# Second dense layer, first half: each weight piece multiplied with two column groups in turn

## The chip, the cores and the metric

The kernel runs on one core of one Trainium2 chip. The metric is the device time of one execution in microseconds. The median of 3 runs before the change is 705.27 us (703.19 to 706.97).

## The reference

Three stages follow each other: attention over a window of 128 keys (batch 4, 8 heads, 576 positions, head size 64), a layer of experts that sends each token to one of 8 experts, and a dense layer. The change lies in the dense layer, which computes on x (2304 tokens by 512):

```python
def _moe2_ref(x, w1, w2, w3, w_out) -> np.ndarray:
    h = np.maximum(np.maximum(x @ w1, x @ w2), x @ w3)
    return (h @ w_out).astype(np.float32)
```

w1, w2 and w3 are 512 by 768, w_out is 768 by 512. They come as float64, and are converted on the core.

## The kernel before

The tokens are worked on in two halves of 1152. For each half the expert layer (`layer1`, two units a half) fills the tile yT, and `layer2(h, ...)` runs the dense layer on it. `layer2` cuts its half into three items of C2 = 384 columns (column groups) and steps the generator `moe2` through them: inner(0), inner(1), outer(0), inner(2), outer(1), outer(2).

*inner(x)* goes over the K2 = 6 blocks m of 128 hidden features, and over the three matrices i. One pair (m, i) is a **product**: 12 matmuls into one bank of PSUM (4 blocks of the 512 inputs, times 3 passes over the high and low f16 parts, each matmul with a weight load of its own and 384 columns). The pool psM has 4 such banks. The result is moved out of PSUM into a tile hx: for i = 0 by ScalarE (L1167), for i = 1 and 2 by VectorE, which takes the maximum with the hx before it (L1169). After i = 2 ScalarE writes the high f16 part of h (L1175) and GpSimd the low part (L1176, yh<-hx,yh). The tag hx has 4 buffers.

*outer(x)* multiplies h with w_out (L1190), scales the rows on ScalarE (L1196) and scatters them to the output (L1197).

The weights of this layer come in 24 pieces of 512 KB: 18 for the pairs (m, i), 6 for w_out. Class `Weights2` handles them. A piece is loaded as int32 words by a transfer on SyncE's queue into a buffer st2 (4 of them; L1065, and L1071 for w_out). VectorE then builds float32 from the words, two pieces at a time, in three steps of two instructions: L1105, L1110, L1116 (the profile shows b<-st and b<-st,b). One call of `tick` emits one step, so three ticks convert a pair of pieces. When the third step is emitted, the transfers for the pair after next are emitted too; they wait until VectorE has released the buffers. `finish` emits, for one piece, ScalarE's scaling and its high f16 part (L1133, L1134), and GpSimd's low part (L1135, g<-b,g or wo<-b,wo). The work is written out in program order and each engine runs its own instructions in that order, so what `tick` emits ahead of a product stands ahead of that product's hx on VectorE. Before each product inner emits ticks by this rule:

```python
for i in range(3):
    if w.done < 3 * (m + 2):
        w.tick()
        w.tick()
    w.tick()
    w.finish()
```

That is three ticks while fewer pieces are converted than two blocks m ahead need, and one tick else; a tick does nothing while more than three converted pieces wait for `finish`.

Each yield of `moe2` returns to `layer2`, which for half 0 advances the gathers of the tokens of the second half (`begin`, `turn`): GpSimd's indirect transfers xg<-xs (L877), ScalarE's and VectorE's split xc<-xg (L899, L900) and SyncE's transposing transfers xh<-xc (L907).

Of the kernel before, what the change touches and what calls it, by code (L numbers as in the profile page):

```python
# [7 lines left out]
F32 = mybir.dt.float32  # L8
# [3 lines left out]
ACTF = mybir.ActivationFunctionType  # L12
ALU = mybir.AluOpType
# [18 lines left out]
KD, KF, K2 = DM // 128, FF // 128, F2 // 128  # L32
# [15 lines left out]
def windowed_attention_moe_kernel(  # L48
# [16 lines left out]
    nc = tc.nc  # L65
# [6 lines left out]
    psM = ctx.enter_context(tc.tile_pool(name="psM", bufs=4, space=PSUM))  # L72
# [4 lines left out]
    xs = [dram.tile([HALF, DM], F32, name=f"xs{h}") for h in range(2)]  # L77
# [171 lines left out]
    fill = Fill()  # L249


    class Attention:
# [26 lines left out]
        def turn(self, nm, b, t, eng=None):  # L279
            a, n = self.raw.pop((nm, b, t)), self.rows(t)  # L280
            ps = psM.tile([128, 4, 128], F32, name="m", tag="m")
            for i in range(4):
                nc.tensor.transpose(  # L283
                    ps[:, i, 0:n], a[0:n, 2 * i:2 * i + 2].rearrange("p h d -> p (h d)"),
                    ident[0:n, 0:n],
                )
            if nm == "k":
                if not t:
                    self.kT[b] = self.p.tile([128, 4, S], F32, name="kT", tag="kT", bufs=2)
                o = self.kT[b][:, :, 128 * t:128 * t + n]  # L290
            else:
                self.qT[b, t] = self.p.tile([128, 4, 128], F32, name="qT", tag="qT", bufs=3)
                o = self.qT[b, t][:, :, 0:n]
            if eng:
                eng.tensor_copy(o, ps[:, :, 0:n])
            else:
                nc.scalar.activation(out=o, in_=ps[:, :, 0:n], func=ACTF.Copy)
# [615 lines left out]
    PASSES = ((0, 0), (0, 1), (1, 0))  # L913
# [130 lines left out]
    class Weights2:  # L1044
# [32 lines left out]
        def begin(self):  # L1077
            g = self.pool.tile([128, 6 * K2 * KD * 128], F16, name="g", tag="g", bufs=1)
            self.g = g.rearrange("p (l i m k c) -> p l i m k c", l=2, i=3, m=K2, k=KD)
# [56 lines left out]

    C2 = 384

    def moe2(pool, items, w, hmt, n2=C2, **kw):

        hms = hmt[:, 0:4 * K2 * C2].rearrange("p (s a f n) -> p s a f n", s=2, a=2, f=K2)
        hms = hms[:, :, :, :, 0:n2]

        def inner(x, yT, c, *_):
            ys = [yT[:, l, :, c:c + n2] for l in range(2)]
            hm = hms[:, x % 2]
            for m in range(K2):
                w.convert(3 * m + 3)
                run = None
                for i in range(3):  # L1150
                    if w.done < 3 * (m + 2):
                        w.tick()
                        w.tick()
                    w.tick()
                    w.finish()
                    ps = psM.tile([128, 512], F32, name="m", tag="m")[:, 0:n2]
                    n = 0
                    for kk in range(KD):
                        for wl, xl in PASSES:
                            nc.tensor.matmul(  # L1160
                                out=ps, lhsT=w.g[:, wl, i, m, kk, :],
                                rhs=ys[xl][:, kk, :], start=(n == 0), stop=(n == 3 * KD - 1),
                            )
                            n += 1
                    nx = pool.tile([128, C2], F32, name="hx", tag="hx", bufs=4)[:, 0:n2]
                    if i == 0:
                        nc.scalar.activation(out=nx, in_=ps, func=ACTF.Copy, scale=2.0 ** -6)  # L1167
                    else:
                        nc.vector.scalar_tensor_tensor(  # L1169
                            out=nx, in0=ps, scalar=2.0 ** -6, in1=run, op0=ALU.mult, op1=ALU.max  # L1170
                        )
                    run = nx
                    fill()
                    fill()
                nc.scalar.activation(out=hm[:, 0, m], in_=run, func=ACTF.Copy)  # L1175
                nc.gpsimd.tensor_tensor(  # L1176
                    out=hm[:, 1, m], in0=run, in1=hm[:, 0, m], op=ALU.subtract
                )
                yield

        def outer(x, yT, c, idxs, gates):
            w.convert(w.n)
            hm = hms[:, x % 2]
            for u in range(n2 // 128):
                t = c // 128 + u
                ps = psM.tile([128, 512], F32, name="m", tag="m")
                n = 0
                for f in range(K2):
                    for wl, xl in PASSES:
                        nc.tensor.matmul(  # L1190
                            out=ps, lhsT=hm[:, xl, f, 128 * u:128 * u + 128],
                            rhs=w.wo[:, wl, f, :], start=(n == 0), stop=(n == 3 * K2 - 1),
                        )
                        n += 1
                ob = pool.tile([128, DM], F32, name="ob", tag="ob", bufs=2)
                nc.scalar.activation(out=ob, in_=ps, func=ACTF.Copy, scale=gates[:, t:t + 1])  # L1196
                nc.gpsimd.indirect_dma_start(  # L1197
                    out=out[:, :],
                    out_offset=bass.IndirectOffsetOnAxis(ap=idxs[:, t:t + 1], axis=0),
                    in_=ob[:, :], in_offset=None, **kw,  # L1200
                )
                yield

        for x, item in enumerate(items):
            yield from inner(x, *item)
            if x:
                yield from outer(x - 1, *items[x - 1])
        yield from outer(len(items) - 1, *items[-1])

    def rest(pool, m2, xT, yT, w, hmt):  # L1210
# [11 lines left out]
        with tc.For_i(0, nx, 1) as i:  # L1222
            far = m2.tile([128, CT], I32, name="far", bufs=1)
            nc.vector.memset(far, 4 * NT)
            for h in range(2):
                wst = Weights(pool, [nc.sync.value_load(
                    rest_e[h][0:1, bass.ds(i, 1)], min_val=0, max_val=E - 1)])
                d = nc.sync.value_load(rest_d[h][0:1, bass.ds(i, 1)], min_val=0, max_val=HALF)
                win = []
                for a, l in zip((gsrc[h], tidx[h], gate[h].bitcast(I32)), lists[h]):  # L1230
                    nc.sync.dma_start(
                        out=l[HALF:WL].rearrange("(t p) o -> p (t o)", p=128), in_=far
                    )
                    nc.sync.dma_start(
                        out=l[0:HALF].rearrange("(t p) o -> p (t o)", p=128), in_=a
                    )
                    w3 = m2.tile([128, CT], I32, name="win", tag="win", bufs=6)
                    nc.sync.dma_start(
                        out=w3, in_=l[bass.ds(d, CX)].rearrange("(t p) o -> p (t o)", p=128)
                    )  # L1240
                    win.append(w3)
                ga = Gather(pool, xT, (nc.sync,))
                for t in range(CT):
                    ga.fetch(xs[h], win[0][:, t:t + 1], t, bounds_check=HALF - 1, oob_is_err=False)
                ga.place(CT)
                ga.send()
                drain(slot(pool, wst, 0, xT, yT, [0, 0, 0], CX))
                drain(moe2(m2, [(yT, 0, win[1], win[2].bitcast(F32))], w, hmt, CX,
                           bounds_check=NT - 1, oob_is_err=False))
# [51 lines left out]
    with tc.manual_schedule():  # L1301
# [30 lines left out]
        yT = [big.tile([128, 2, KD, WY], F16, name="yT0", bufs=1)]  # L1332
# [5 lines left out]
        bats, w2s, m2 = [], None, None  # L1338
# [90 lines left out]

        def layer2(h, hmt):  # L1430
            items = [(yT[h], c, tidx[h], gate[h]) for c in range(0, HALF, C2)]
            for i, _ in enumerate(moe2(m2, items, w2s, hmt)):
                if h == 0:
                    begin()
                    turn()
                    if i >= 12:
                        wst.issue(27)
                    if i >= 20:
                        wst.low(25)
                        wst.high(26)  # L1440
# [8 lines left out]
        xa_cm.__exit__(None, None, None)  # L1449
        yb = ctx.enter_context(tc.tile_pool(name="yb", bufs=1))  # L1450
        layer2(0, yb.tile([128, 2 * KD * WY], F16, name="yh", tag="yh", bufs=1))
        while not bats[3].done:
            wait(3, TILES[3])
# [8 lines left out]
        hmt = m2.tile([128, 2 * KD * WH], F16, name="xh", tag="xh", bufs=1)  # L1462
# [36 lines left out]
```

## Time and profile before

| what | value |
|---|---|
| median of 3 runs | 705.27 us (703.19 to 706.97) |
| profiled execution, its own time | 707.38 us |
| span of the profile | 705.5 us |
| PE (TensorE matmul) busy | 648.6 us, 92% of the span |
| PEld (weight load) busy | 400.8 us, 57% |
| DVE (VectorE) busy | 354.4 us, 50% |
| ACT (ScalarE) busy | 346.6 us, 49% |
| POOL (GpSimd) busy | 225.7 us, 32% |
| granted TensorE clock, mean | 0.98 |

The profile is of one execution; its times are in us from the start of the span, mean durations in ns. The span is 1.9 us shorter than that execution's own time. Shares are averages over stages with different limits. A matmul's duration of some 326 ns overlaps the next one's, so the rate of matmuls is read from stretches, not from single durations. "x168" in a row is a count; in square brackets stands how long the engine sat idle ahead of the row and which instruction ended that.

### The profile page before, as it was taken

Reading aid. Unit: us, or ns where it says so; the run is one execution under the profiler, and the core shown is the slowest. Engines: PE = TensorE matmul, PEld = TensorE weight load, DVE = VectorE, ACT = ScalarE, POOL = GpSimd, SP = SyncE. Lnnn points to the kernel's source line nnn. Section 1 sums busy time; section 2 is a strip of 40 time slices with the busy share of each in tenths; the row PEclk is TensorE's granted clock in tenths of the full one; section 3 lists DMA queues with packets and bytes.
Section 4 is the critical chain, followed back from the end, with each engine's and each line's share of the span. In section 5 each row is a group of like instructions: output and inputs, shape, how many; then the busy total and the mean of one; then the engine's idle time right before and its main releaser. Section 6 shows DMA issues by size and latency. Waiting matters only on the chain.

```text
span 705.5 us, 12899 instructions
## 1 busy us (share of the span) xinstructions
PE 648.6 (92%) x4787; PEld 400.8 (57%) x4787; DVE 354.4 (50%) x1083; ACT 346.6 (49%) x660; POOL 225.7 (32%) x232
## 2 busy tenths in 40 slices
PE   6899878989897999896799999999999999999993
PEld 5687755556664656653455565444447766655641
DVE  5977764665466739999952134052223355201100
ACT  5898867767685727654541221264656311111110
POOL 2111216323221315666652311292334211121121
PEclk9999989999999999999999999999999999999997
DMA  9656754445430247775623502253331000000011
GB/s 191 103 121 142 206 144 110 105 121 135 112 103 25 76 133 249 215 233 179 178 59 47 119 22 76 88 172 112 105 104 31 2 0 1 1 25 22 0 46 48
DMA packets 120800, 69.95 MB, mean 99 GB/s; under 512 B 68872, under 2 KB 115484, under 8 KB 120732
## 3 DMA queue, kind: packets, MB, share of 16 engines
q1 hardware_dynamic: 116992, 59.06, 31.7%
q0 software_dynamic: 3040, 9.96, 4.7%
q8 instruction: 40, 0.66, 0.4%
q14 instruction: 28, 0.23, 0.1%
q10 hardware_dynamic: 700, 0.04, 0.1%
HBM read 57.19 MB, written 9.44 MB: 94 GB/s over the span
## 4 chain that ended last, share of the span: by engine, by line
PE 71%; DVE 15%; ACT 6%; DMA 3%; issue 3%; POOL 0%; ACTq 0%; DVEq 0%; POOLq 0%; SPq 0%
PE m L1160 24%; PE m L991 12%; PE m L1010 12%; PE m L1190 9%; PE s L335 4%; PE m L376 2%; PE m L468 2%; DVE b L1110 2%; PE bank L406 2%; PE m L283 2%; DVE wt L963 2%; DMA st<-in_moe_w_dram 2%; DVE e L348 2%; ACT e L357 2%; DVE b L1105 1%
## 5 line engine op out<-in xcount | busy, mean ns | idle before, releaser
L1160 PEld LDWEIGHTS <-g 128*128 128x128 f16 x1296 | 127.4, 99 | 103.2 <-issue 17.2
L1160 PE MATMUL m<-yT,g 128*128 128x384 f16 x648 | 111.3, 332 | 14.6 <-DVE hx L1169 9.1
L1160 PE MATMUL m<-yh,g 128*128 128x384 f16 x648 | 105.7, 326 | 0.0
L1010 PE MATMUL m<-ht,wt 128*128 128x496 f16 (+3 forms) x576 | 101.3, 335 | 2.6 <-DVE el L387 1.2
L1169 DVE SCALAR_TENSOR_TENSOR hx<-m,hx 128x384 f32<-128x384 f32 x72 | 40.0, 555 | 124.1 <-PE m L1160 122.7
L963 DVE SCALAR_TENSOR_TENSOR wt<-st,wt 128x1024 f16<-128x1024 f32 x48 | 61.9, 1293 | 79.2 <-ACT wt L954 79.2
L991 PEld LDWEIGHTS <-wt 128*128 128x128 f16 x576 | 55.4, 98 | 54.8 <-issue 8.3
L1010 PEld LDWEIGHTS <-wt 128*128 128x128 f16 x576 | 54.8, 99 | 45.0 <-issue 4.8
L983 POOL TENSOR_TENSOR ht<-hf,ht 128x496 f16<-128x496 f32 (+3 forms) x48 | 49.2, 1029 | 87.8 <-ACT ht L982 85.0
L981 ACT ACTIVATE hf<-m 128x496 f32<-128x496 f32 (+3 forms) x72 | 35.8, 498 | 74.7 <-PE m L1010 47.8
L357 ACT ACTIVATE e<-e,nm 128x256 f32<-128x256 f32 (+2 forms) x144 | 59.5, 471 | 22.5 <-DVE nm L348 22.3
L991 PE MATMUL m<-xT,wt 128*128 128x496 f16 (+2 forms) x288 | 57.9, 344 | 6.8 <-DVE el L387 3.8
L348 DVE CUSTOM_DVE_ANT_0 e<-s,bias 128x256 f32<-128x256 f32 (+1 forms) x128 | 45.8, 382 | 19.5 <-PE s L335 11.4
L954 ACT ACTIVATE wt<-st 128x1024 f16<-128x1024 f32 x48 | 50.0, 1045 | 3.5 <-DMA st<-in_moe_w_dram 3.4
L991 PE MATMUL m<-xh,wt 128*128 128x496 f16 (+1 forms) x288 | 51.1, 330 | 0.0
L387 DVE TENSOR_TENSOR el<-m,eh 128x512 f16<-128x512 f32 x64 | 42.3, 682 | 7.0 <-ACT eh L382 7.0
L335 PE MATMUL s<-kT,qT 64*128 64x256 f32 (+2 forms) x320 | 42.3, 384 | 3.3 <-DVE nm L348 2.2
L1176 POOL TENSOR_TENSOR xh<-hx,xh 128x384 f16<-128x384 f32 x18 | 16.4, 914 | 89.8 <-ACT xh L1175 89.8
L311 POOL TENSOR_TENSOR vl<-rawv,vh 128x512 f16<-128x512 f32 (+1 forms) x20 | 23.0, 1149 | 68.8 <-ACT vh L304 68.8
L1175 ACT ACTIVATE xh<-hx 128x384 f16<-128x384 f32 x18 | 9.4, 523 | 71.1 <-DVE hx L1169 67.1
L1196 ACT ACTIVATE ob<-m,gate 128x512 f32<-128x512 f32 x18 | 12.4, 687 | 55.0 <-PE m L1190 49.6
L376 PE MATMUL m<-ident,e 128*128 128x128 f32 (+1 forms) x256 | 35.9, 279 | 1.4 <-issue 0.8
(184 smaller groups left out, 977.6 us busy)
## 6 DMA issues: line engine op xcount, KB each, us to landing
st<-in_moe_w_dram SPq DMA_DIRECT2D x66, 512.0 KB
rawk<-in_k_dram SPq DMA_DIRECT2D x16, 256.0 KB
rawq<-in_q_dram SPq DMA_DIRECT2D x16, 256.0 KB
rawv<-in_v_dram SPq DMA_DIRECT2D x16, 256.0 KB
xs<-x SPq DMA_DIRECT2D x16, 256.0 KB
st<-in_moe_w_out_dram SPq DMA_DIRECT2D x6, 512.0 KB
rawk<-in_k_dram SPq DMA_DIRECT2D x4, 128.0 KB
rawq<-in_q_dram SPq DMA_DIRECT2D x4, 128.0 KB
```

The lines of the kernel that those rows point to most:

```text
L335: nc.tensor.matmul(out=out[u][rows, x // 2, c0:c1], lhsT=self.qT[b, t][r, i, 0:n], rhs=self.kT[b][r, i, k0 + c0:k0 + c1], start=True, stop ...
L348: nc.vector.tensor_tensor_reduce(out=e[:, x, c0:c1], in0=s[x % 2][:, x // 2, c0:c1], in1=bias[:, x, c0:c1], scale=-0.125, scalar=3.0e38, o ...
L357: nc.scalar.activation(out=e[:, x, c0:c1], in_=e[:, x, c0:c1], func=ACTF.Exp, scale=-1.0, bias=nm[:, x:x + 1],)
L376: nc.tensor.transpose(ps[:n, x, :], e[:, x, a:z], ident)
L387: nc.vector.tensor_tensor(out=o, in0=a, in1=b, op=ALU.subtract)
L954: nc.scalar.activation(out=wt[:, 0], in_=st, func=ACTF.Copy, scale=SW)
L963: nc.vector.scalar_tensor_tensor(out=wt[:, 1], in0=st.rearrange("p (a b) -> p a b", a=a), scalar=SW, in1=wt[:, 0], op0=ALU.mult, op1=ALU.s ...
L983: nc.gpsimd.tensor_tensor(out=lo, in0=hf, in1=hi[1], op=ALU.subtract)
L991: nc.tensor.matmul(out=ps, lhsT=wt[:, wl, kk, o:o + 128], rhs=xT[:, xl, kk, bass.ds(d[0], cap)], start=(n == 0), stop=(n == 3 * KD - 1),)
L1010: nc.tensor.matmul(out=ps, lhsT=wt[:, wl, f, :], rhs=hs[f][:, xl], start=(n == 0), stop=(n == 3 * KF - 1),)
L1160: nc.tensor.matmul(out=ps, lhsT=w.g[:, wl, i, m, kk, :], rhs=ys[xl][:, kk, :], start=(n == 0), stop=(n == 3 * KD - 1),)
L1190: nc.tensor.matmul(out=ps, lhsT=hm[:, xl, f, 128 * u:128 * u + 128], rhs=w.wo[:, wl, f, :], start=(n == 0), stop=(n == 3 * K2 - 1),)
```

## The change

In half 0 (`both=h == 0`) inner now takes several items. For each pair (m, i) it runs the product of column group 0 and then that of column group 1, each with ticks and a `finish` by the same rule ahead of it, and keeps a running hx for each group. After the three i it splits h for group 0 and for group 1, with one yield behind each. The order of a half is then: inner(0 and 1), outer(0), inner(2), outer(1), outer(2). In half 1 inner gets one item, and the order is as before.

```diff
-                for i in range(3):
-                    if w.done < 3 * (m + 2):
+                run = {}
+                for i in range(3):
+                    for x in xs:
+                        if w.done < 3 * (m + 2):
+                            w.tick()
+                            w.tick()
                         w.tick()
-                        w.tick()
-                    w.tick()
-                    w.finish()
...
+                        w.finish()
+                        run[x] = product(run.get(x), *items[x][0:2], m, i)
+                        fill()
+                        fill()
+                for x in xs:
+                    hm = hms[:, x % 2]
+                    nc.scalar.activation(out=hm[:, 0, m], in_=run[x], func=ACTF.Copy)
+                    nc.gpsimd.tensor_tensor(
+                        out=hm[:, 1, m], in0=run[x], in1=hm[:, 0, m], op=ALU.subtract
+                    )
+                    yield
...
-        for x, item in enumerate(items):
-            yield from inner(x, *item)
-            if x:
-                yield from outer(x - 1, *items[x - 1])
+        x0 = 2 if both else 1
+        yield from inner(*range(x0))
+        for x in range(x0, len(items)):
+            if both and x == 2:
+                yield from outer(0, *items[0])
+            yield from inner(x)
+            yield from outer(x - 1, *items[x - 1])
         yield from outer(len(items) - 1, *items[-1])
...
-            for i, _ in enumerate(moe2(m2, items, w2s, hmt)):
+            for i, _ in enumerate(moe2(m2, items, w2s, hmt, both=h == 0)):
```

`product` holds the 12 matmuls and the move out of PSUM, as they were. Its lines are L1150 (matmul), L1157 and L1159 (hx on ScalarE and VectorE); the split is L1180 and L1181.

On VectorE, in the second block m of the first inner, before (two pairs of pieces; b64 are the words of a piece being converted, m a bank of PSUM, hx the running maximum):

```order
L1105 TENSOR_SCALAR b64_4771<-st2_4685 128x512
L1105 TENSOR_SCALAR b64_4772<-st2_4687 128x512
L1110 SCALAR_TENSOR_TENSOR b64_4771<-st2_4685,b64_4771 128x512
L1110 SCALAR_TENSOR_TENSOR b64_4772<-st2_4687,b64_4772 128x512
L1116 SCALAR_TENSOR_TENSOR b64_4771<-st2_4685,b64_4771 128x512
L1116 SCALAR_TENSOR_TENSOR b64_4772<-st2_4687,b64_4772 128x512
L1105 TENSOR_SCALAR b64_4801<-st2_4733 128x512
L1105 TENSOR_SCALAR b64_4802<-st2_4735 128x512
L1169 SCALAR_TENSOR_TENSOR hx_4821<-m_4808,hx_4799 128x384
L1110 SCALAR_TENSOR_TENSOR b64_4801<-st2_4733,b64_4801 128x512
L1110 SCALAR_TENSOR_TENSOR b64_4802<-st2_4735,b64_4802 128x512
L1169 SCALAR_TENSOR_TENSOR hx_4841<-m_4828,hx_4821 128x384
```

The same place now:

```order
L1159 SCALAR_TENSOR_TENSOR hx_4900<-m_4887,hx_4858 128x384
L1105 TENSOR_SCALAR b64_4902<-st2_4806 128x512
L1105 TENSOR_SCALAR b64_4903<-st2_4808 128x512
L1159 SCALAR_TENSOR_TENSOR hx_4922<-m_4909,hx_4876 128x384
L1110 SCALAR_TENSOR_TENSOR b64_4902<-st2_4806,b64_4902 128x512
L1110 SCALAR_TENSOR_TENSOR b64_4903<-st2_4808,b64_4903 128x512
L1159 SCALAR_TENSOR_TENSOR hx_4939<-m_4926,hx_4900 128x384
L1116 SCALAR_TENSOR_TENSOR b64_4902<-st2_4806,b64_4902 128x512
L1116 SCALAR_TENSOR_TENSOR b64_4903<-st2_4808,b64_4903 128x512
L1159 SCALAR_TENSOR_TENSOR hx_4963<-m_4950,hx_4922 128x384
```

Four hx stand in a block m where two stood, and one conversion step stands between two of them.

On VectorE where the conversions end, before:

```order
L1169 SCALAR_TENSOR_TENSOR hx_5128<-m_5115,hx_5106 128x384
L1110 SCALAR_TENSOR_TENSOR b64_5108<-st2_5056,b64_5108 128x512
L1110 SCALAR_TENSOR_TENSOR b64_5109<-st2_5058,b64_5109 128x512
L1169 SCALAR_TENSOR_TENSOR hx_5148<-m_5135,hx_5128 128x384
L1116 SCALAR_TENSOR_TENSOR b64_5108<-st2_5056,b64_5108 128x512
L1116 SCALAR_TENSOR_TENSOR b64_5109<-st2_5058,b64_5109 128x512
L1169 SCALAR_TENSOR_TENSOR hx_5188<-m_5175,hx_5170 128x384
```

The same place now (xc is the gather's split):

```order
L900 TENSOR_TENSOR xc_5235<-xg_4975,xc_5235 128x512
L900 TENSOR_TENSOR xc_5238<-xg_4977,xc_5238 128x512
L1105 TENSOR_SCALAR b64_5249<-st2_5152 128x512
L1105 TENSOR_SCALAR b64_5250<-st2_5154 128x512
L1110 SCALAR_TENSOR_TENSOR b64_5249<-st2_5152,b64_5249 128x512
L1110 SCALAR_TENSOR_TENSOR b64_5250<-st2_5154,b64_5250 128x512
L1116 SCALAR_TENSOR_TENSOR b64_5249<-st2_5152,b64_5249 128x512
L1116 SCALAR_TENSOR_TENSOR b64_5250<-st2_5154,b64_5250 128x512
L1159 SCALAR_TENSOR_TENSOR hx_5306<-m_5293,hx_5269 128x384
```

Before, the hx behind the last step is that of product 23 of half 0 (counted from 1); now it is that of product 27, the first of block m = 4 that VectorE moves out, and a second pair of xc stands ahead of the last conversion. TensorE's instructions stand in the same sequence of shapes in both kernels; which weights and columns they read differs.

## Rows read from the trace of the kernel before

**Rows 1.** Page, part 2: PE and DVE, busy tenths in 40 slices of the span.
```profile
PE   6899878989897999896799999999999999999993
...
DVE  5977764665466739999952134052223355201100
```

**Rows 2.** Busy time of each engine in two stretches of 10 us.
```profile
345.00:355.00 10.00, 6.54 (x39) 3.69 (x38) 10.00 (x12) 4.64 (x9) 6.88 (x5) 1.00 0.58 156
355.00:365.00 10.00, 9.45 (x58) 5.60 (x58) 5.59 (x9) 6.26 (x12) 6.18 (x6) 1.00 0.22 50
```

**Rows 3.** Timeline, PE, 305 to 386 us: start, length, instruction, count, idle before.
```profile
305.01 14.11 PE L1160 MATMUL m<-yT,g 128*128 128x384 f16 x84
...
333.57 5.80 PE L1160 MATMUL m<-yT,g 128*128 128x384 f16 x26 [2.65 <-DVE hx L1169]
...
357.66 27.46 PE L1160 MATMUL m<-yT,g 128*128 128x384 f16 x168 [0.25 <-ACT hx L1167]
```

**Rows 4.** Groups by line, 301.4 to 356.44 us: count, busy us, mean ns, idle before.
```profile
L1160 PE MATMUL m<-yT,g 128*128 128x384 f16 x243 | 43.6, 336 | 12.0 <-DVE hx L1169 9.1 <-POOL g L1135 2.5 <-ACT hx L1167 0.3
...
L1135 POOL TENSOR_TENSOR g<-b,g 128x512 f16<-128x512 f32 x14 | 19.7, 1414 | 9.5 <-ACT g L1134 9.3
...
L1176 POOL TENSOR_TENSOR yh<-hx,yh 128x384 f16<-128x384 f32 x6 | 7.2, 1208 | 6.3 <-ACT yh L1175 6.2
L1169 DVE SCALAR_TENSOR_TENSOR hx<-m,hx 128x384 f32<-128x384 f32 x12 | 6.5, 544 | 0.0
L1135 POOL TENSOR_TENSOR wo<-b,wo 128x512 f16<-128x512 f32 x4 | 5.6, 1399 | 5.1 <-ACT wo L1134 5.0
L877 POOL DMA_INDIRECT xg<-xs,r_gidx x4 | 4.2, 1056 | 0.9 <-issue 0.6 <-POOL yh L1176 0.2
```

**Rows 5.** Timeline, DVE, 300 to 357 us.
```profile
300.20 1.27 DVE L1116 SCALAR_TENSOR_TENSOR b<-st,b 128x512 int32<-128x512 int32 x2
301.40 0.74 DVE L1105 TENSOR_SCALAR b<-st 128x512 int32<-128x512 int32 x2
302.08 1.27 DVE L1110 SCALAR_TENSOR_TENSOR b<-st,b 128x512 int32<-128x512 int32 x2
303.28 0.54 DVE L1169 SCALAR_TENSOR_TENSOR hx<-m,hx 128x384 f32<-128x384 f32 x1
303.75 2.74 DVE L1116 SCALAR_TENSOR_TENSOR b<-st,b 128x512 int32<-128x512 int32 x2
...
336.79 1.59 DVE L900 TENSOR_TENSOR xc<-xg,xc 128x512 f16<-128x512 f32 x2 [1.11 <-ACT xc L899]
...
339.10 3.74 DVE L1110 SCALAR_TENSOR_TENSOR b<-st,b 128x512 int32<-128x512 int32 x2
...
355.17 1.27 DVE L1116 SCALAR_TENSOR_TENSOR b<-st,b 128x512 int32<-128x512 int32 x2
```

**Rows 6.** Timeline, POOL, near 340 us.
```profile
340.01 2.27 POOL L1135 TENSOR_TENSOR g<-b,g 128x512 f16<-128x512 f32 x2
```

**Rows 7.** Lines L1135 and L1176, whole span: ns min/median/max, first and last start us.
```profile
L1135 POOL TENSOR_TENSOR g<-b,g x18: 1150/1502/2192, 273.9 to 341.1; 128x512 f16<-128x512 f32 x18
...
L1176 POOL TENSOR_TENSOR yh<-hx,yh x18: 902/916/1450, 307.6 to 433.2; 128x384 f16<-128x384 f32 x18
```

**Rows 8.** Line L1160, 294 to 305 us, columns as in the rows above.
```profile
L1160 PE MATMUL m<-yT,g x36: 322/326/527, 294.4 to 304.6; 128*128 128x384 f16 x36
```

**Rows 9.** Chain of work that ended last, in order of time: start, length, what.
```profile
344.54 4.68 DMA st<-in_moe_w_out_dram
...
357.66 27.46 PE m L1160 x168
385.12 11.65 PE m L1190 x54
...
671.03 19.44 PE m L1190 x90
```

More of the change, by code (lines that the diff above doesn't have):

```diff
@@ L1137, in windowed_attention_moe_kernel, with moe2, product, inner @@
     C2 = 384
-    def moe2(pool, items, w, hmt, n2=C2, **kw):
+    def moe2(pool, items, w, hmt, n2=C2, both=False, **kw):
         hms = hmt[:, 0:4 * K2 * C2].rearrange("p (s a f n) -> p s a f n", s=2, a=2, f=K2)
         hms = hms[:, :, :, :, 0:n2]
-        def inner(x, yT, c, *_):
-            ys = [yT[:, l, :, c:c + n2] for l in range(2)]
-            hm = hms[:, x % 2]
+        def product(run, yT, c, m, i):
+            ps = psM.tile([128, 512], F32, name="m", tag="m")[:, 0:n2]
+            n = 0
+            for kk in range(KD):
+                for wl, xl in PASSES:
+                    nc.tensor.matmul(
+                        out=ps, lhsT=w.g[:, wl, i, m, kk, :],
+                        rhs=yT[:, xl, kk, c:c + n2], start=(n == 0), stop=(n == 3 * KD - 1),
+                    )
+                    n += 1
+            nx = pool.tile([128, C2], F32, name="hx", tag="hx", bufs=4)[:, 0:n2]
+            if i == 0:
+                nc.scalar.activation(out=nx, in_=ps, func=ACTF.Copy, scale=2.0 ** -6)
+            else:
+                nc.vector.scalar_tensor_tensor(
+                    out=nx, in0=ps, scalar=2.0 ** -6, in1=run, op0=ALU.mult, op1=ALU.max
+                )
+            return nx
+        def inner(*xs):
@@ L1147, in inner @@
             for m in range(K2):
                 w.convert(3 * m + 3)
-                run = None
+                run = {}
                 for i in range(3):
-                    if w.done < 3 * (m + 2):
+                    for x in xs:
+                        if w.done < 3 * (m + 2):
+                            w.tick()
+                            w.tick()
                         w.tick()
-                        w.tick()
-                    w.tick()
-                    w.finish()
[L1156 to L1179, printed above, removed]
+                        w.finish()
[7 more added lines that the diff above has]
+                        out=hm[:, 1, m], in0=run[x], in1=hm[:, 0, m], op=ALU.subtract
+                    )
+                    yield
```

## The prediction

> **What bounds the kernel now.** I read the page first, then the stretch that the change touches. On the page TensorE shows an 8 or 9 in nearly all slices of the middle, but in slices 19 and 20 it falls to 6 and 7, at the end of five nines of VectorE (slices 16 to 20) [rows 1]: for once VectorE is the full engine. That is the first inner of half 0. The table of stretches shows it: from 345 to 355 us VectorE is busy 10.00 of 10.00 us and TensorE 6.54; from 355 to 365 us VectorE falls to 5.59 and TensorE rises to 9.45 [rows 2]. The groups by line then tell what TensorE waits for between 301.4 and 356.44 us: 12.0 us of idle time ahead of its matmuls, 9.1 of them ended by an hx of VectorE, 2.5 by a low part of a weight piece on GpSimd [rows 4]. The timeline of TensorE has these waits as single rows (2.65 us behind an hx at 333.57), and behind 357.66 there are 168 matmuls in 27.46 us without a gap [rows 3]. 168 matmuls are 14 products, so a product costs TensorE 27.46 / 14 = 1.96 us when nothing holds it, and 36 - 14 = 22 of the 36 products of the first two column groups are done at 357.66.
>
> So VectorE sets this stretch. It converts nine pairs of weight pieces from 301.40 to 356.44 us, when the last step ends (355.17 + 1.27) [rows 5]. From there the chain of waits is TensorE's: 27.46 us of products, the first outer at 385.12, and products and outers up to 671.03 + 19.44 [rows 9]. What is won before 385.12 moves the end, if nothing behind it is late.
>
> **What the change does not do.** Each matmul keeps a weight load of its own, since the second column group runs as 12 more matmuls and not inside the first's. TensorE's instruction counts stay. Its time alone is not shortened; what changes is how many products are ready while VectorE converts.
>
> **The sum.** In the first inner TensorE has one product for each piece that VectorE converts, afterwards two. The question is when VectorE ends its last conversion, and how many products are left for TensorE then.
>
> *Uncontended prices* [rows 5]: a step of L1105 takes 302.08 - 301.40 = 0.68 us from start to next start, L1110 303.28 - 302.08 = 1.20, L1116 301.40 - 300.20 = 1.20. A pair costs 3.08. An hx costs 303.75 - 303.28 = 0.47. A visit of the gather (two xc with the wait for ScalarE ahead) costs 1.11 + 1.59 = 2.70.
>
> *Before:* the 55.04 us from 301.40 to 356.44 hold nine pairs (27.72), 12 hx [rows 4] (5.64) and one visit (2.70). That is 36.06; 18.98 us are missing. They lie in single conversion steps that are far longer than their clean length: 2.74 us for a L1116 step at 303.75, 3.74 us for the L1110 at 339.10 [rows 5]. In that last one GpSimd runs two low parts, 340.01 to 342.28 [rows 6]. GpSimd's subtractions hold VectorE up. In the stretch there are 14 + 4 of L1135 and six of L1176 [rows 4], the last of which only starts in VectorE's last step; 18.98 / 23 = 0.83 us for each. The hx, with 544 ns on average over 12 [rows 4], is not slowed.
>
> *After:* by the order of VectorE nine pairs stand there again, but 16 hx (four in each of the blocks m = 0 to 3) and two visits. GpSimd runs the same 18 low parts and 8 yh. The sum is 27.72 + 16 x 0.47 (7.52) + 2 x 2.70 (5.40) + 26 x 0.83 (21.58) = 62.2 us. The last conversion ends at 301.4 + 62.2 = 363.6, 7.2 us later than before. Next on VectorE stands the hx of product 27 (0.54); with four banks of PSUM, product 31 is the first that needs it. Products 31 to 36 start at 364.2 and take 6 x 1.96 = 11.8, to 376.0. Before, the first outer began at 385.12. **The gain is 9.1 us**: 8 products fewer are left (15.7 us), and the conversions end later by nearly half of that.
>
> *Bounds of the one unknown price,* GpSimd's hold on VectorE. At zero VectorE would be done long before; then TensorE's own rate bounds. At 305.01, 36 matmuls, 3 products, are done [rows 8], and the other 33 take 64.7 us, to 369.7: a gain of 15.4. At the other end each subtraction holds VectorE for all of its own shortest length, 1.15 us for the 18 and 0.90 for the 8 [rows 7]: 27.9 in place of 21.6 us, a gain of 2.8. I take 0.83, the mean of the same instructions in the same stretch.
>
> The Trainium skill, SBUF — State Buffer, section "Who interferes with whom", calls the port pair that VectorE and GpSimd share an exclusive lock: a VectorE instruction with two SBUF inputs and a GpSimd instruction that reads SBUF block one another for a whole instruction, and a VectorE instruction with at most one SBUF input outside the 2-port modes is not touched. The trace agrees on the hx, which reads one PSUM bank and one SBUF tile, and on the 3.74 us step. By that rule the added yh speak against this change, since each may cost its full length; taken to the end the sum is the 2.8 us above.
>
> *What goes along.* TensorE starts this inner as before; the short waits ahead of 305 us are for the expert layer's last output and stay. A transfer of a piece starts when VectorE releases its buffer and lands 4.68 us later [rows 9]; between the release by one pair and the need by the pair after next lies the whole pair between, at least 3.08 us, two hx and its share of GpSimd's hold (2 to 3 subtractions, some 2 us), so it lands in about the time that VectorE needs. ScalarE's `finish` and moves stand behind the steps that they wait for anyway. SyncE's last two w_out transfers stand behind two transposing transfers now; these wait for the first visit's xc, which is done two blocks m earlier. The first outer needs all of w_out, converted by 364 and used at 376; it needs the last yh of group 0 for its last block of features only. From there on each engine's order is the old one but for the gather's place between hx; TensorE bounds there, so I cost this at nothing, and if a gather were late, TensorE would stop at the start of half 1.
>
> **The rivals.**
>
> *TensorE becomes the bound (14%).* GpSimd's subtractions fall between the hx, which they do not slow, as one conversion step now stands between two hx. Below 15.4 us of hold in all (0.59 each) VectorE's last step ends by 357.4 and product 31 never waits. For it: hx are a larger part of VectorE's work. Against it: VectorE has no slack in the stretch [rows 2], so that GpSimd nearly always meets a conversion. Time: 705.27 - 15.4 = 689.9.
>
> *The stretch grows as much as the backlog shrinks (10%).* VectorE is as full as before, and the waits of its own queue add to the locks: ScalarE stands longer behind `finish` ahead of the xc, and a pair's transfer lands late. With the full lock (gain 2.8) and no other wait the time is 702.5; one us of late landing more in two of the nine pairs gives 704.5. Against it: the 18.98 us already contain what such waits cost before.
>
> *Slower (6%): the ring of four hx.* The final hx of group 0 must be read by GpSimd before VectorE can write the hx four products later, which is now the next block's i = 1 of the same group; before, it was the block after. If GpSimd is late, VectorE stands, and with it the conversions queued behind. At m = 0 two gather issues of 1.06 us [rows 4] stand between the two yh, with low parts around them. The wait begins when GpSimd ends a yh later than a pair and two hx (about 6 us with its holds) behind the final hx. It decides against the change from 9.1 / 4 = 2.3 us at each of the four block ends; at 3.3 us each the time is 705.27 + 4.1 = 709.4. Against it: GpSimd is busy 6.88 of 10 us at the fullest [rows 2] and waits for ScalarE, not the reverse [rows 4].
>
> **The numbers.** The forecast case, VectorE-bound with a gain of 9.1, has 70%. The sum is made against the profiled execution, 707.38 us; the median is 2.1 lower, and I take the gain off the median: 705.27 - 9.1 = **696.2 us**. The range goes from the TensorE-bound 689.9 to 701.0, which is a hold of 1.02 us for each subtraction; some 2 in 10 lie outside, nearly all above. A measurement of this kernel tells about 0.5%, 3.5 us, from no change. Faster by more: 0.84 (the forecast and the first rival); within: 0.10; slower by more: 0.06.
>
> **What would show it.** Right: VectorE full from 301 us to about 363, with 16 hx and two visits in it; TensorE's idle time in that stretch about 6 us and spread over the hx; about 72 matmuls left when the last conversion ends; the first outer near 376; from there the same lengths as before. Wrong: waits of TensorE for a weight piece's g, idle time of VectorE ahead of L1105 that a transfer ends, or ahead of an hx that GpSimd ends; conversions that end before 357 (the first rival) or after 370; or a stop of TensorE at the start of half 1.

## The result and the profile after

The changed kernel takes 693.45 us (median of 4 runs, 692.74 to 693.81); the kernel before takes 704.29 beside it (median of 4, 703.19 to 706.97). The ratio is 0.9839, with a 95% interval of 0.9807 to 0.9871: 10.8 us less, 9.1 to 13.6 by the interval. The forecast was 696.2 with a range of 689.9 to 701.0.

The profiled execution took 693.81 us with a span of 691.9, at a mean granted clock of 0.983. The page's 40 slices, against [rows 1]: slices 19 and 20 of TensorE read 9 and 8 where they read 6 and 7, and VectorE's full stretch has moved with the conversions.

```profile
PE   6899888989997999899889999999999999999993
...
DVE  5977864666475738999981233152324455201100
```

Busy time in three stretches of 10 us (PE, PEld, DVE, ACT, POOL, then granted clock and DMA), against [rows 2]. VectorE is still full, and TensorE is busy 9.54 of 10 us beside it; before it was 6.54. Only at the end of the conversions does it fall to 7.46, and then nothing holds it.

```profile
340.00:350.00 10.00, 9.54 (x59) 5.55 (x57) 10.00 (x13) 4.16 (x8) 6.52 (x5) 1.00 0.89 215
350.00:360.00 10.00, 7.46 (x46) 4.28 (x45) 8.72 (x12) 6.61 (x13) 8.40 (x7) 1.00 0.42 102
360.00:370.00 10.00, 10.00 (x63) 5.99 (x62) 2.51 (x6) 2.60 (x5) 3.17 (x4) 1.00 0.01 2
```

TensorE's timeline of the first inner and the first outer (L1195), against [rows 3]:

```profile
290.47 1.30 PE L1150 MATMUL m<-yT,g 128*128 128x384 f16 x7
...
301.13 25.51 PE L1150 MATMUL m<-yT,g 128*128 128x384 f16 x156
326.90 4.06 PE L1150 MATMUL m<-yT,g 128*128 128x384 f16 x24 [0.25 <-ACT hx L1157]
332.36 4.06 PE L1150 MATMUL m<-yT,g 128*128 128x384 f16 x24 [1.40 <-DVE hx L1159]
336.63 4.06 PE L1150 MATMUL m<-yT,g 128*128 128x384 f16 x24 [0.21 <-DVE hx L1159]
341.00 12.17 PE L1150 MATMUL m<-yT,g 128*128 128x384 f16 x72 [0.31 <-ACT hx L1157]
354.46 4.06 PE L1150 MATMUL m<-yT,g 128*128 128x384 f16 x24 [1.29 <-ACT hx L1157]
359.77 11.86 PE L1150 MATMUL m<-yT,g 128*128 128x384 f16 x72 [1.25 <-DVE hx L1159]
371.46 11.82 PE L1195 MATMUL m<-wo,yh 128*128 128x512 f16 x54
```

The waits behind 301.13 are 0.25 + 1.40 + 0.21 + 0.31 + 1.29 + 1.25 = 4.7 us, all for an hx; before, the groups had 12.0 [rows 4]. When the last one ends, 72 matmuls are left, 6 products; before it was 168, 14 products.

The same two places in the timeline of the kernel before:

```profile
294.36 1.30 PE L1160 MATMUL m<-yT,g 128*128 128x384 f16 x7
...
384.95 11.82 PE L1190 MATMUL m<-wo,yh 128*128 128x512 f16 x54
```

From the first product of the inner to the first matmul of the outer it is 371.46 - 290.47 = 81.0 us; before, 384.95 - 294.36 = 90.6. (The 385.12 of [rows 9] is from the chain, where a row starts when the one before it has ended; the chain of the changed kernel has 371.63. The expectations below say 90.8, which mixes the two views.) From there to the end of the span it is 691.9 - 371.46 = 320.4 us and before 705.5 - 384.95 = 320.5. So the changed stretch gives 9.6 us and nothing behind it takes any of it back. The spans differ by 13.6 us. Of the rest, 3.9 lie ahead of the changed code, where these two executions happen to differ: the inner began at 290.47 here and at 294.36 before, and between 288.0 and 295.4 in the executions of the experiments. The experiments are therefore read by the length of this stretch, beside their times.

The groups by line from 297.51, where the second pair's conversion starts, to 359.25, where the last step ends (61.74 us), against [rows 4]:

```profile
L1150 PE MATMUL m<-yT,g 128*128 128x384 f16 x341 | 57.7, 330 | 3.6 <-ACT hx L1157 1.9 <-DVE hx L1159 1.6
...
L1110 DVE SCALAR_TENSOR_TENSOR b<-st,b 128x512 int32<-128x512 int32 x18 | 17.2, 997 | 0.0
L1116 DVE SCALAR_TENSOR_TENSOR b<-st,b 128x512 int32<-128x512 int32 x19 | 16.6, 910 | 0.0
L1105 DVE TENSOR_SCALAR b<-st 128x512 int32<-128x512 int32 x18 | 13.5, 788 | 0.1
...
L1159 DVE SCALAR_TENSOR_TENSOR hx<-m,hx 128x384 f32<-128x384 f32 x17 | 9.3, 548 | 0.5 <-PE m L1150 0.5
...
L900 DVE TENSOR_TENSOR xc<-xg,xc 128x512 f16<-128x512 f32 x4 | 4.7, 1224 | 3.0 <-ACT xc L899 3.0
```

TensorE now starts 341 matmuls while VectorE converts, not 243. VectorE waits for ScalarE's part of the gather (3.0 us) and, at the first hx, 0.5 us for TensorE, else 0.1 us in all. The hx stay at 548 ns, the steps are at 788 to 997 ns on average, and the xc (L900) at 1224.

### The profile page after: what moved, and what is told of

It reads as the page before. It is cut to its first block, busy times and chain, and to the rows that moved or that the text cites. A ratio compares the mean times of both kernels' runs of the same rounds, so it can differ in the third digit from the quotient of the medians.

```text
span 691.9 us, 12893 instructions
## 1 busy us (share of the span) xinstructions
PE 645.2 (93%) x4787; PEld 400.0 (58%) x4787; DVE 353.6 (51%) x1083; ACT 345.3 (50%) x660; POOL 226.6 (33%) x232
## 4 chain that ended last, share of the span: by engine, by line
PE 73%; DVE 12%; ACT 6%; DMA 3%; issue 3%; POOL 0%; ACTq 0%; SPq 0%; POOLq 0%; DVEq 0%
PE m L1150 25%; PE m L991 13%; PE m L1010 12%; PE m L1195 10%; PE s L335 4%; DMA st<-in_moe_w_dram 2%; PE m L376 2%; PE m L468 2%; DVE b L1110 2%; PE m L283 2%; PE bank L406 2%; DVE e L348 2%; ACT e L357 2%; ACT eh L382 1%; DVE wt L963 1%
## 5 line engine op out<-in xcount | busy, mean ns | idle before, releaser
L1150 PEld LDWEIGHTS <-g 128*128 128x128 f16 x1296 | 127.2, 98 | 93.8 <-issue 11.3
L1150 PE MATMUL m<-yT,g 128*128 128x384 f16 x648 | 109.1, 329 | 7.3 <-DVE hx L1159 2.9
L1150 PE MATMUL m<-yh,g 128*128 128x384 f16 x648 | 105.7, 326 | 0.0
L1159 DVE SCALAR_TENSOR_TENSOR hx<-m,hx 128x384 f32<-128x384 f32 x72 | 39.7, 555 | 116.7 <-PE m L1150 116.7
L983 POOL TENSOR_TENSOR ht<-hf,ht 128x496 f16<-128x496 f32 (+3 forms) x48 | 49.5, 1036 | 89.3 <-ACT ht L982 85.7
L348 DVE CUSTOM_DVE_ANT_0 e<-s,bias 128x256 f32<-128x256 f32 (+1 forms) x128 | 45.8, 382 | 19.9 <-PE s L335 11.7
L1181 POOL TENSOR_TENSOR xh<-hx,xh 128x384 f16<-128x384 f32 x18 | 16.4, 913 | 89.8 <-ACT xh L1180 89.8
L1180 ACT ACTIVATE xh<-hx 128x384 f16<-128x384 f32 x18 | 9.4, 523 | 70.8 <-DVE hx L1159 66.9
L382 ACT ACTIVATE eh<-m 128x512 f16<-128x512 f32 x64 | 34.6, 584 | 4.3 <-PE m L376 4.1
```

Source lines behind the costliest of these rows:

```text
L348: nc.vector.tensor_tensor_reduce(out=e[:, x, c0:c1], in0=s[x % 2][:, x // 2, c0:c1], in1=bias[:, x, c0:c1], scale=-0.125, scalar=3.0e38, o ...
L382: nc.scalar.activation(out=b, in_=a, func=ACTF.Copy)
L983: nc.gpsimd.tensor_tensor(out=lo, in0=hf, in1=hi[1], op=ALU.subtract)
L1150: nc.tensor.matmul(out=ps, lhsT=w.g[:, wl, i, m, kk, :], rhs=yT[:, xl, kk, c:c + n2], start=(n == 0), stop=(n == 3 * KD - 1),)
```

## The experiments

The theory: VectorE's conversions bound the first inner, GpSimd's subtractions lengthen them, and TensorE's backlog when they end is what the change shortens. The rivals: GpSimd does not matter; the gain is that TensorE has work to do whatever VectorE does; the gain is that conversion runs further ahead; the ring of hx binds. Unless a diff says otherwise, an experiment is an edit of the changed kernel. "Conversions" goes from the second pair's L1105 to the last L1116, "steps busy" adds the three groups L1105, L1110 and L1116 of that stretch, "inner" goes from its first product to the first matmul of the outer. Experiments 1 to 5 and 8 are one execution each, 6 and 9 are four and 7 is six; of these the time is the median.

| kernel | time (before beside it), us | conversions | steps busy | inner |
|---|---|---|---|---|
| before | 704.29 | 55.0 | 49.2 | 90.6 |
| changed | 693.45 (704.29) | 61.7 | 47.3 | 81.0 |
| 1 no low part of h by GpSimd | 694.79 (708.22) | 57.1 | 43.1 | 77.3 |
| 2 no low part of the weights by GpSimd | 692.25 (708.22) | 58.9 | 32.1 | 79.9 |
| 3 the same in the kernel before | 694.90 (708.22) | 48.2 | 31.9 | 82.3 |
| 4 ring of eight hx | 697.09 (708.22) | 61.7 | 47.0 | 81.0 |
| 5 before, two steps ahead of each product | 715.41 (706.84) | 54.9 | 45.7 | 100.7 |
| 6 steps ahead of the first group only | 691.54 (706.84) | 71.2 | 42.1 | 75.0 |
| 7 five single steps in six products | 687.29 (706.84) | 65.9 | 44.4 | 75.0 |
| 8 as 2, steps from the second i on | 688.72 (702.81) | 56.7 | 33.6 | 77.0 |
| 9 one step for each product, from the third on | 692.13 (702.81) | 61.0 | 48.0 | 80.0 |

**1. GpSimd's 8 subtractions for h.**

```diff
-                    nc.gpsimd.tensor_tensor(
-                        out=hm[:, 1, m], in0=run[x], in1=hm[:, 0, m], op=ALU.subtract
-                    )
+                    if both and len(xs) == 2:
+                        nc.scalar.activation(
+                            out=hm[:, 1, m], in_=run[x], func=ACTF.Copy, scale=0.0
+                        )
+                    else:
...
```

> Leaves out the low part of h for the first two column groups of half 0: ScalarE writes zeros there, where GpSimd subtracted. All else is as in the changed kernel. Measures: the inner (first product of the first inner to first matmul of the first outer), 90.8 us before and 81.0 us in the changed kernel; the conversions (second pair's L1105 to the last L1116), 55.0 and 61.7 us. Theory (a GpSimd subtraction holds VectorE for 0.83 us): 8 of 26 holds go, conversions 61.7 - 6.6 = 55 us, TensorE's own rate then bounds, inner 75 to 77 us, time 688 to 690. Rival (GpSimd's work does not matter, VectorE's own instructions fill the stretch): conversions 61 to 62, inner 81, time 693.

The groups of the conversions (302.46 to 359.60 us) in this kernel:

```profile
L1110 DVE SCALAR_TENSOR_TENSOR b<-st,b 128x512 int32<-128x512 int32 x18 | 16.2, 940 | 0.0
L1116 DVE SCALAR_TENSOR_TENSOR b<-st,b 128x512 int32<-128x512 int32 x19 | 14.1, 777 | 0.0
L1105 DVE TENSOR_SCALAR b<-st 128x512 int32<-128x512 int32 x18 | 12.8, 745 | 0.2 <-DMA st<-in_moe_w_dram 0.2
...
L900 DVE TENSOR_TENSOR xc<-xg,xc 128x512 f16<-128x512 f32 x4 | 2.6, 695 | 4.2 <-ACT xc L899 4.2
```

The same 55 instructions of the steps take 43.1 us where they took 47.3, and the four xc 2.6 us where they took 4.7. So GpSimd instructions on other tiles lengthen VectorE's; the rival by which GpSimd doesn't matter falls. VectorE's busy time falls by 4.2 + 2.1 = 6.3 us, 0.79 for each of the 8 subtractions, near the 0.83 of the forecast. The conversions are only 4.6 us shorter (57.1, not 55) because VectorE now waits longer: 4.2 us for ScalarE ahead of the xc, 1.2 more than in the changed kernel (ScalarE also writes the zeros), and 0.5 more in other places. The inner is 3.7 us shorter, 77.3 us where 75 to 77 was expected; the time of 694.79 belongs to an execution whose inner began at 295.41, 4.9 us later than the changed kernel's.

**2. The weights' low parts,** in `finish`:

```diff
-            nc.gpsimd.tensor_tensor(out=dst[1], in0=b, in1=dst[0], op=ALU.subtract)
+            nc.scalar.activation(out=dst[1], in_=b, func=ACTF.Copy, scale=0.0)
```

> Leaves out the low parts of all 24 weight pieces of the dense layer: ScalarE writes zeros there, where GpSimd subtracted. Theory: 18 of 26 holds go, conversions 61.7 - 15 = 47 us, the clean steps show (0.68, 1.20, 1.20 from start to start); inner 75 to 77 us as in the run with 8 holds gone, since TensorE's rate bounds both; time 688 to 690. Rival (long steps come from transfers or from ScalarE, not from GpSimd): steps as long as before, conversions 58 to 62.

Its groups (295.44 to 354.34 us):

```profile
L1110 DVE SCALAR_TENSOR_TENSOR b<-st,b 128x512 int32<-128x512 int32 x18 | 12.2, 720 | 0.0
L1116 DVE SCALAR_TENSOR_TENSOR b<-st,b 128x512 int32<-128x512 int32 x19 | 12.2, 678 | 0.0
...
L1159 DVE SCALAR_TENSOR_TENSOR hx<-m,hx 128x384 f32<-128x384 f32 x17 | 9.4, 552 | 13.1 <-PE m L1150 12.2 <-ACT g L1135 0.7
...
L1105 DVE TENSOR_SCALAR b<-st 128x512 int32<-128x512 int32 x18 | 7.7, 462 | 0.9 <-DMA st<-in_moe_w_out_dram 0.9
```

The steps take 32.1 us, 15.2 less than in the changed kernel: 0.84 us for each of 18 subtractions, as the theory has it. The hx are 552 ns, as ever. Yet the conversions last 58.9 us, since VectorE now waits 12.2 us for TensorE ahead of its hx. TensorE has become the bound: after its start it runs the remaining 33 products without a gap. The inner is still longer than the 75 to 77 us expected.

```profile
299.12 6.58 PE L1150 MATMUL m<-yT,g 128*128 128x384 f16 x26 [5.57 <-POOL yT L983]
...
305.79 64.51 PE L1150 MATMUL m<-yT,g 128*128 128x384 f16 x396
370.13 10.09 PE L1195 MATMUL m<-wo,yh 128*128 128x512 f16 x46
```

What I had not foreseen is the first row: TensorE stands 5.57 us for the expert layer's last low part, a GpSimd subtraction (L983). It took 6.26 us; the shortest of the same shape takes 0.64. In that time VectorE's timeline is an unbroken row of steps:

```profile
294.23 1.27 DVE L1116 SCALAR_TENSOR_TENSOR b<-st,b 128x512 int32<-128x512 int32 x2
295.44 0.74 DVE L1105 TENSOR_SCALAR b<-st 128x512 int32<-128x512 int32 x2
296.11 1.27 DVE L1110 SCALAR_TENSOR_TENSOR b<-st,b 128x512 int32<-128x512 int32 x2
297.31 1.27 DVE L1116 SCALAR_TENSOR_TENSOR b<-st,b 128x512 int32<-128x512 int32 x2
```

The reading that VectorE's steps keep GpSimd out, as GpSimd's keep VectorE out, is tested in 8.

**3. The same edit in the kernel before,** with its single column group.

> The kernel before, with the low parts of all 24 weight pieces of the dense layer left out in the same way. Theory: the stretch before was VectorE's, and a third of it holds: conversions 55.0 - 15 = 40 us, TensorE nearly at its rate, inner 76 to 78 us, time 690 to 692, so that even without the second column group the gain of the change would be there. Rival (in the old order TensorE waits for each weight piece's arrival, whatever VectorE's load): inner 86 us or more.

```profile
297.97 7.17 PE L1160 MATMUL m<-yT,g 128*128 128x384 f16 x26 [4.37 <-POOL yT L983]
...
345.31 27.46 PE L1160 MATMUL m<-yT,g 128*128 128x384 f16 x168 [0.43 <-ACT hx L1167]
```

The conversions take 48.2 us, not 55.0, and the inner 82.3, not 90.6, even with 4.37 us of the new stop at the start in it. The expected 40 and 76 to 78 us were missed: VectorE now waits 6.0 us for TensorE and 4.2 us for transfers of weight pieces. The old order without GpSimd's load gets most of what the change gets. The edit also takes away the waits of TensorE for low parts from GpSimd (2.5 us before [rows 4]), so not all of these 8.3 us is VectorE's. TensorE's backlog is still 14 products, but its last row begins 55.0 us after the start of the inner, where it was 357.66 - 294.36 = 63.3: an earlier end of VectorE gains with no change in the backlog. The rival by which VectorE's price doesn't matter (86 or more) falls.

**4. The ring of hx.**

```diff
-            nx = pool.tile([128, C2], F32, name="hx", tag="hx", bufs=4)[:, 0:n2]
+            nx = pool.tile([128, C2], F32, name="hx", tag="hx", bufs=8)[:, 0:n2]
```

> The changed kernel with 8 buffers of hx in place of 4. Theory: the ring does not bind, inner 81 us (80.5 to 81.5), conversions 61 to 62.5. Rival (what TensorE still waits for after the change is hx that GpSimd releases late): inner 78 us or less.

Conversions of 61.7 us and an inner of 81.0, with the same six waits (TensorE's last row begins with `[1.24 <-DVE hx L1159]`). The ring binds nothing. The time, 697.09, is above the changed kernel's because this execution began its inner at 293.86, 3.4 us later.

**5. Conversion further ahead, in the kernel before.** The rule for the steps and `finish` stands twice ahead of each product:

```diff
-                    if w.done < 3 * (m + 2):
...
+                    for _ in range(2):
+                        if w.done < 3 * (m + 2):
+                            w.tick()
+                            w.tick()
```

> The kernel before, one column group after another, with the ticks and the finish ahead of each product run twice: the conversion steps per product of the old order, doubled, which is the other half of what the change does (its ticks run for two products of each piece). Theory (what counts is how many products are left when VectorE ends): conversions end 2.5 us sooner (52.5 us, 8 hx in them in place of 12), but with 19 products left and not 14, so inner 90.8 + 9.8 - 2.5 = 98 us, time 710 to 713. Rival (the change gains since pieces are converted further ahead): inner 81 to 85, time 694 to 698.

```profile
302.77 6.58 PE L1161 MATMUL m<-yT,g 128*128 128x384 f16 x26 [5.70 <-POOL yT L983]
...
354.46 38.89 PE L1161 MATMUL m<-yT,g 128*128 128x384 f16 x228 [2.88 <-DVE hx L1170]
393.18 7.07 PE L1191 MATMUL m<-wo,yh 128*128 128x512 f16 x32
```

715.41 us, 8.6 more than before. The conversions last as long as before, 54.9 us and not the 52.5 expected, but 17 products are done beside them and 19 are left (228 matmuls). The last wait ends 62.0 us after the start of the inner (63.3 before), and then 11 us more of products follow: the inner is 10 us longer. Of these 11, 1.6 are TensorE's clock: behind the wait of 2.88 us the granted clock was 0.50 (the 1.2 GHz level) from 356 to 358 us, and the 228 matmuls took 38.89 us where 27.46 for 168 gives 37.3. A part of the 10 us is the stop of 5.70 us for L983, in which VectorE converts and TensorE does nothing; how much of the 10 us that makes was not separated. At most it is the 6.3 us by which the first 3 products came later than before; with these and the clock taken off the inner would still be 92.8 us, not the 81 to 85 of the rival. Running ahead by itself is no gain, and here a loss. The change gains because it lets *more products* run per conversion step.

**6. and 7. Spreading the steps further.** By the theory the best is a conversion that ends just as TensorE ends. In 6 the steps stand ahead of the first group's products only:

```diff
+                        if x == xs[0]:
+                            if w.done < 3 * (m + 2):
+                                w.tick()
+                                w.tick()
...
```

> The changed kernel with ticks ahead of the first column group's product alone, so as many steps per weight piece as before. VectorE has 24 hx, 12 in place of 8 yh and 3 visits of the gather in the stretch, and the last steps stand at its end. Theory: TensorE at its rate in the inner, 75 to 78 us, but 1 to 3 us of wait in the first outer for the last pieces of w_out; time 689 to 692. Rival (steps must run ahead, or TensorE waits for g): waits of TensorE for g of several us, time 695 or more.

```profile
298.65 64.51 PE L1150 MATMUL m<-yT,g 128*128 128x384 f16 x396
362.99 2.75 PE L1196 MATMUL m<-wo,yh 128*128 128x512 f16 x12
366.93 0.59 PE L1196 MATMUL m<-wo,yh 128*128 128x512 f16 x2 [1.18 <-ACT wo L1134]
368.53 10.31 PE L1196 MATMUL m<-wo,yh 128*128 128x512 f16 x40 [1.01 <-POOL wo L1135]
378.68 6.50 PE L1150 MATMUL m<-yT,g 128*128 128x384 f16 x39
```

The inner is at TensorE's rate, 75.0 us, but the conversions go on beyond it, and the first outer, which needs all of w_out, takes 378.68 - 362.99 = 15.7 us where it takes 11.7 in the changed kernel. 4.0 us go back, more than expected. The waits are 1.18 + 1.01 = 2.2 us of it; behind them the granted clock, 1.00 till then, was 0.50 from 369 to 371 us, and the last 40 matmuls took 10.31 us where the changed kernel's 11.82 for 54 gives 8.8. Ratio 0.9808 (0.9749 to 0.9868), which doesn't tell it from the changed kernel. In 7 each block has five single steps for six products:

```diff
+                        if len(xs) == 2:
+                            if (i, x) != (2, xs[1]):
+                                w.tick()
+                        else:
...
```

> The changed kernel with one tick ahead of five of every six products of the first inner, so that the ten pairs end with product 33 and not 26. Theory: VectorE's work is spread over the whole inner: 21 hx in the conversions, 27.7 + 9.9 + 5.4 + 28 x 0.83 = 66 us; then TensorE's rate bounds, inner 75 to 78 us, time 689 to 691, 3 to 5 us under the changed kernel. Rival (the sum over the inner is VectorE's in any order): inner 80 to 82, time 693.

```profile
297.28 6.07 PE L1150 MATMUL m<-yT,g 128*128 128x384 f16 x26 [1.83 <-POOL yT L983]
...
303.44 64.51 PE L1150 MATMUL m<-yT,g 128*128 128x384 f16 x396
367.78 11.82 PE L1199 MATMUL m<-wo,yh 128*128 128x512 f16 x54
```

The inner is 75.0 us, and the outer has no wait. VectorE converts until 365.76 us, 2 us ahead of the first outer, and in its groups its hx wait for TensorE:

```profile
L1159 DVE SCALAR_TENSOR_TENSOR hx<-m,hx 128x384 f32<-128x384 f32 x22 | 11.9, 550 | 7.0 <-PE m L1150 6.8
```

687.29 us (6 runs, 684.96 to 689.87), ratio 0.974 with an interval of 0.9694 to 0.9787. It beats both kernels; against the changed one its inner is 6.0 us shorter.

**8. The stop at the start.** As 2, but without steps ahead of the first two products (m = 0, i = 0):

```diff
+                        if len(xs) == 1 or m or i:
+                            if w.done < 3 * (m + 2):
+                                w.tick()
+                                w.tick()
...
```

> The run without the low parts of the weight pieces (ScalarE writes zeros there), and besides no tick ahead of the first two products. Open from that run: TensorE stopped 5.57 us near its start behind one GpSimd subtraction of the expert layer (L983) that took 6.26 us. Theory: the hold works both ways, and VectorE's unbroken row of conversion steps kept GpSimd out; two steps fewer in that row (2.4 us) let it end 2.4 us sooner: L983 3.5 to 4.2 us, TensorE's stop 2.8 to 3.5 us, inner 77 to 78 us. Rival (that subtraction is late for another reason): L983 still about 6 us, inner 80.

GpSimd's row with the held subtraction, first in 2 and then here (the second instruction of each is the held one):

```profile
291.00 8.07 POOL L983 TENSOR_TENSOR yT<-hf,yT 128x224 f32 x2 [4.37 <-ACT yT L982]
```

```profile
289.76 5.66 POOL L983 TENSOR_TENSOR yT<-hf,yT 128x224 f32 x2 [4.37 <-ACT yT L982]
```

With the steps ahead of the first two products put off, GpSimd's row is 2.4 us shorter and TensorE's stop falls from 5.57 to 3.16. The inner falls from 79.9 to 77.0, as expected. In both runs the held instruction ends 0.49 us behind VectorE's last step: at 299.07 for 297.31 + 1.27 = 298.58 in 2, and at 295.42 for 294.93 here. So VectorE's steps hold GpSimd up too.

**9. Both at once:** one step for each product, none ahead of the first two.

```diff
+                        if len(xs) == 2:
+                            if m or i:
+                                w.tick()
+                        else:
...
```

> The changed kernel with no tick ahead of the first two products and one tick ahead of each of the other 34. Theory: VectorE's row of steps ahead of its first hx has three steps fewer than in the changed kernel, L983 takes 0.7 to 1.5 us and TensorE's stop behind it is at most 1.3 us; TensorE's rate bounds the rest; inner 74 to 75.5 us, time 685 to 689, the same as the run with five ticks in six within what a measurement tells. Rival (five ticks in six was faster only since it converted less per product): inner 77 or more.

```profile
294.23 6.07 PE L1150 MATMUL m<-yT,g 128*128 128x384 f16 x26 [1.35 <-POOL yT L983]
...
352.42 17.44 PE L1150 MATMUL m<-yT,g 128*128 128x384 f16 x96 [2.37 <-ACT hx L1157]
369.70 11.82 PE L1199 MATMUL m<-wo,yh 128*128 128x512 f16 x54
```

The stop at the start shrinks to 1.35 us, but the inner is 80.0 us and the time 692.13 (ratio 0.9855, 0.9839 to 0.9872), no better than the changed kernel's. My expectation of 74 to 75.5 was wrong and its rival held: TensorE waits again, 2.37 us behind an hx at 350 us. The trace leads that wait back to VectorE, which is busy 10.00 of 10.00 us from 340 to 350. It ran two xc in 2.25 us from 347.81 (0.7 us each where nothing holds them, experiment 1) and only then, at 349.99, the L1116 that a `finish` on ScalarE waited 2.25 us for; TensorE's hx stands behind that `finish`. Behind the wait the granted clock was 0.50 from 353 to 355 us, and the 96 matmuls took 17.44 us where 27.46 for 168 gives 15.7. So the 5.0 us more than in 7 are some 2.6 of waits and 1.7 of clock, and the rest is not accounted for. My reading is that five steps for six products leave VectorE the slack that one for one does not; putting off the visit of the gather alone was not tested.

## Why the prediction was right

*VectorE bounds the stretch, and the price of its work.* The forecast put the conversions at 62.2 us; they took 61.74. The clean part held: experiment 2 shows the steps near their clean price when GpSimd's load is gone. The held part was 21.58 us by forecast. Measured, 61.74 - 27.72 - 7.52 leaves 26.5 for visits and holds together, where the forecast had 27.0. The two visits cost 4.7 + 3.0 = 7.7 us, not 5.4: 0.8 of the difference is longer waits for ScalarE, the rest is longer xc, which GpSimd holds up as it does the steps (1224 ns each, 695 without its 8 subtractions for h). With 3.6 us of waits, 2.8 for four xc at 695 ns and 0.3 for two small instructions of the gather taken off, 19.8 us are hold, 0.76 for each of 26 subtractions. By VectorE's busy time experiment 1 gives 0.79 for one of h and the steps of experiment 2 give 0.84 for one of the weights. Together these make 6.3 + 15.2 = 21.5 us, more than 19.8, so they don't simply add. The forecast's 0.83 was near, a little too high; that the conversions came out within 0.5 us is in part luck, since the visits were priced too low.

*The backlog.* 6 products left in place of 14, as forecast: 15.7 us. The last wait ends at 359.77, which from the start of the inner is 69.3 us, where the kernel before got to its last row after 357.66 - 294.36 = 63.3: 6.0 us later. 15.7 - 6.0 = 9.7 us, the gain of the stretch within 0.1 us; the forecast had 9.1. The first outer was forecast near 376; with this execution's earlier start taken out it is 371.63 + 3.89 = 375.5, by the chain as in the forecast.

*TensorE's waits* are 4.7 us where I had some 6. They are for hx, as the theory wants, and none for a weight piece's g. The prediction says nothing of TensorE's clock. That cost it nothing: at the start of the inner the granted clock fell to 0.50 in both kernels, and from 300 us to the first outer it was 1.00 in the changed one. Before, it was 0.50 from 333 to 336 us, behind the wait of 2.65 us, but TensorE stood again after that, for a low part on GpSimd.

*The rest at nothing.* From the first outer to the end it is 320.4 us, before 320.5.

*The median.* The forecast took 9.1 from 705.27. The measured 693.45 is 2.7 us lower; of this 0.5 is the stretch (9.6 for 9.1), and 1.0 is that the kernel before has a median of 704.29 beside the changed one. The other 1.2 lies in what differs from execution to execution: the interval of the gain, 9.1 to 13.6, covers it.

*The rivals.* TensorE as the bound didn't come about, because GpSimd's hold was 19.8 us, not below 15.4; experiment 7 shows TensorE as the bound, with an inner of 75.0. That the stretch would grow as much as the backlog shrinks needed the full lock, 27.9 us; the measured hold is 19.8. The ring of hx plays no part (experiment 4). What the prediction did not price is the hold in the other direction: it treats GpSimd as the one that holds up VectorE, and costs the start of the inner at nothing. In the changed kernel that was right within a microsecond (its waits there are 0.52 + 0.78 + 1.10, before 0.52 + 1.38 + 0.51), but where the steps run unbroken at that point it costs 3 to 6 us (experiments 2, 3, 5 and 8).

## What to carry to other kernels

When one engine prepares operands and another uses them, count at the moment when the first ends how much is left for the second: that backlog is paid in full, so a reorder that lets the consumer work meanwhile may gain even when it makes the producer end later (its conversions took 61.7 us and not 55.0, for 15.7 us less of backlog). Pace the producer to end just ahead of the consumer, with a little slack: five steps for six products made 75.0 us of 81.0, a step for every product made 80.0, and ending beyond the consumer gave 4.0 us back. And a subtraction put on an idle GpSimd is not free: where VectorE is full, price it as a part of VectorE's time, some 0.8 us for each here.

## What was not expected of the hardware

The two engines hold each other up for a run of instructions, not only for one. In the changed kernel one L1105 step of VectorE, else 0.37 us of busy time (0.74 for two [rows 5]), lasts 5.06 us:

```profile
313.90 5.06 DVE L1105 TENSOR_SCALAR b<-st 128x512 int32<-128x512 int32 x1
```

Beside it GpSimd is first in a gather issue (L877, 313.45 to 314.40), then runs four subtractions one after the other, and VectorE comes in when they end (315.29 + 3.38 = 318.67; the step ends at 318.96):

```profile
314.42 0.93 POOL L1181 TENSOR_TENSOR yh<-hx,yh 128x384 f16<-128x384 f32 x1
315.29 3.38 POOL L1135 TENSOR_TENSOR g<-b,g 128x512 f16<-128x512 f32 x3
```

It cost TensorE nothing there: its 156 matmuls from 301.13 on run through. In the other direction it is the 6.26 us of L983 in experiment 2. The Trainium skill, SBUF — State Buffer, section "Who interferes with whom", calls this an exclusive lock that is held for a whole instruction. Both directions agree with a lock, though here it keeps the other engine out for a run of instructions. The held L1105 reads a single SBUF tile; the section has such an instruction held only in a 2-port mode, and no run here shows its mode. The hx agree too, which read one PSUM bank and one SBUF tile and stay between 544 and 552 ns on average in every group shown. The profile counts the time of being held as busy: VectorE reads 10.00 of 10.00 us between 340 and 350, although the same steps without GpSimd's weight parts take a third less.

A stop of TensorE can also cost more than its length, as in experiments 5, 6 and 9: the granted clock was 0.50 for some us behind it, and 1.5 to 1.7 us went that way.
